# Polynomial attention and a blend of experts on one core: the first unit's queries by token, the third unit's rows behind the weights, the first copy of v in halves

## The chip, the cores and the metric

The program runs on one core of a Trainium2 chip. A core has five engines with a queue of instructions each: TensorE (PE; its weight loads are shown apart as PEld), VectorE (DVE), ScalarE (ACT), GpSimd (POOL) and SyncE (SP), which here issues nearly all transfers between the chip's memory and the core's. An engine takes its instructions strictly in the order of the program; between engines, semaphores say when something is done. The metric is the device time of one execution in microseconds (us); shown is the median of five.

## What is computed

Two blocks after one another, cut to what matters:

```python
# q, k, v: (4, 4, 1088, 32);  S1, S2: (8, 32)
def phi(x):                                  # 64 features of a row
    a = einsum('rd,bhsd->bhsr', S1, x)       # 8 numbers
    b = einsum('rd,bhsd->bhsr', S2, x)       # 8 numbers
    return einsum('bhsi,bhsj->bhsij', a, b)  # all 64 products
kv = einsum('bhsf,bhsd->bhfd', phi(k), v)
z  = phi(k).sum(axis=2)
x  = (phi(q) @ kv) / (phi(q) . z + 1e-6)     # then (b, h, s, d) -> (b*s, h*d): 4352 rows of 128

p = domain_probs / (domain_probs.sum(-1) + 1e-9)        # 4352 x 4
out = sum over e of p[:, e] * (relu(x @ w1[e]) @ w2[e]) # 4 experts, 128 -> 1024 -> 128
```

There is no softmax: a batch's keys and values shrink to one 64 x 33 table per head (kv and z), and each query is then a product with that table.

## The kernel before

**Order of the whole.** The 4352 tokens are cut into chunks of columns of x (128, 448, 512, five more of 512, 320, 256, 128), and a chunk goes through 16 steps, four for each expert: `first` multiplies by w1 and rectifies, `second`, two steps later, multiplies by w2. The attention makes x (`xT`, 128 features by 4352 tokens) in units of a batch: batch 0 in units of 128, 448 and 512 tokens. The order is written out by hand: `start()` makes keys, kv and the first unit of batch 0, and all later attention is cut into small pieces, which `work()` puts between the steps. So only the work of `start()` stands ahead of TensorE's expert products.

**Transfers (lines 85 to 163).** SP issues, in this order: S2, the keys of batch 0 (`kn`, 544 KB), q's first 128 columns (`qn`, 64 KB), v in four transfers of 128 KB and two of 16 KB, q's columns 128 to 1088 (480 KB; these are the second and third unit), w1[0], five small ones of domain_probs, w2[0], then w1 and w2 of experts 1 to 3, each 512 KB. Eight semaphores go round over the transfers, so that a transfer is issued only when the one eight before it has landed.

**Preparation.** VectorE decodes S (given as 64-bit words) into `s_T`, 32 x 64, by some fourteen small instructions. From it ScalarE and GpSimd lay out `sk`, the projection for the keys: 128 x 128, by head, S1 in one half and S2 in the other. They also lay out `sp` and from it `sr`, six 128 x 128 matrices, which are S1 and S2 with their rows already repeated in the order of the 64 products.

**`start()` (lines 674 to 733).** VectorE turns the rows of k (`kT`) and of the first 128 queries (`qT`) by blocks of 32. TensorE projects the keys in three groups of token tiles (0 to 3, 4 to 7, 8), token by feature, into PSUM tiles named `h`; ScalarE copies each group to `fs` (line 360). The products of the 64 features (`key_product`, line 391) are made by VectorE for the first pair of heads and by GpSimd for most of the second, into `kp`. ScalarE copies v into `vx`, which has a column of ones for z, in two copies of four tiles (line 337) and one of the last half tile (line 342). Then TensorE sums: `key_sum`, 36 instructions (72 records in the trace, where one instruction of this type shows as two) into one PSUM tile `f`, first tiles 0 to 3 for both pairs of heads, then 4 to 8.

The first unit's queries stand between the projections of the keys and the key sum. TensorE multiplies `qT` by the six matrices of `sr`, feature by token: the result in `o0` is the second factor of all products, that in `o1` and `num` the first factors. ScalarE copies `o0` to `qb`, and four VectorE products of 64 x 128 (line 501) give `qp`, 128 features by 128 tokens for each pair of heads.

At the end VectorE turns the second unit's rows (line 488, one instruction of 256 columns and one of 192), `key_divide` makes `kvz` from `f` between the two, TensorE multiplies `kvz` and `qp` to denominators (`den`) and numerators (`num`), VectorE divides into `xT` in two halves, and the expert products begin (`h` from `xT` and `w_sb`). The program's names w1_sb and w2_sb both show as `w_sb`. For chunk 0 the steps alternate on TensorE: eight records `h`, eight records `o`. Step 8 is the first that uses w1 of expert 2.

Of the kernel before, what the change touches and what calls it, by code (L numbers as in the profile page):

```python
# [8 lines left out]
F32 = mybir.dt.float32  # L9
BF16 = mybir.dt.bfloat16  # L10
I32 = mybir.dt.int32
ALU = mybir.AluOpType
# [4 lines left out]
def _ap(t, p0: int, np_: int, off: int, free):  # L17

    p = list(t.ap)[0]
    return bass.AP(t.tensor, t.offset + p0 * p[0] + off, [[p[0], np_]] + [list(d) for d in free])  # L20
# [3 lines left out]
def kernel(  # L24
# [24 lines left out]
    nc = tc.nc  # L49

    P = 128
# [32 lines left out]
    def psum(pool, tag):  # L84
        return pool.tile([P, 512], F32, tag=tag, name=tag)


    def load_rows(src, b, name, part=slice(0, S)):

        d = kn if name == "kn" else qn  # L90
        if b not in d:
            d[b] = lpool.tile([P, S], F32, tag=name, bufs=2, name=name)
        c, n = part.start, part.stop - part.start
        base = src.offset + b * H * S * D
        if name == "qn" and b == B - 1:
            for c, n, t in ((0, (G - 4) * D, 0), ((G - 4) * D, 4 * D, S - P)):
                nc.sync.dma_start(d[b][:, c : c + n], bass.AP(src.tensor, base + t * D, [[S * D, H], [n, 32], [1, n]]))
        else:
            nc.sync.dma_start(d[b][:, part], bass.AP(src.tensor, base + c, [[G * D, P], [1, n]]))  # L99
# [32 lines left out]
    def load_w2(e):  # L132
        nc.sync.dma_start(w2_sb[:, e], w2[e].rearrange("(f p) d -> p f d", p=P))  # L133
# [11 lines left out]

    ends = cpool.tile([P, 2, E], F32, name="ends")
    e_sum = cpool.tile([P, 2, 3], F32, name="e_sum")
    load_rows(q, 0, "qn", slice(P, S))
    load_w1(0)
    for p0, n, g0, m, t in ((0, 96, 0, G, 0), (96, 32, 0, G - 4, 3 * S), (96, 32, G - 4, 4, B * S - P)):  # L150
        nc.sync.dma_start(
# [8 lines left out]
    for e in range(1, E):  # L160
        load_w1(e)
        load_w2(e)
    sk = cpool.tile([P, P], F32, name="sk")
    sp = cpool.tile([32, 3, 2, 32], F32, name="sp")
    sr = cpool.tile([P, 3, 2, P], F32, name="sr")
    sq = cpool.tile([P, P], F32, name="sq")
    nc.gpsimd.memset(sk[:, :], 0.0)
    nc.gpsimd.memset(sr[:, :, :, :], 0.0)
    nc.gpsimd.memset(sq[:, :], 0.0)
    kT = cpool.tile([P, P * NT], F32, name="kT")  # L170
    nc.gpsimd.memset(kT[:, S:], 0.0)
# [6 lines left out]
    for h in range(H):  # L178
        nc.gpsimd.memset(own2[32 * h : 32 * h + 32, h % 2 : h % 2 + 1], 1.0)


    eps = cpool.tile([P, 1], F32, name="eps")
    nc.gpsimd.memset(eps[:, :], 0.0)
# [20 lines left out]
    def both(out, weights, moving, **flags):  # L204

        for _ in range(2):
            on_side(lambda s: out[half[s], :], lambda s: weights[:, half[s]], lambda s: moving, **flags)
# [34 lines left out]

    def copy_on(scalar):
        return nc.scalar.copy if scalar else nc.gpsimd.tensor_copy

    for h in range(H):
        copy_on(h < 2)(_ap(sk, 32 * h, 32, R2 * h, [[HP, 2], [1, R2]]), _ap(s_T, 0, 32, 0, [[D, 2], [1, R2]]))  # L250
    for i in range(3):
        copy_on(i == 2)(
            _ap(sp, 0, 32, HP * i, [[32, 2], [R, 4], [1, R]]),
            _ap(s_T, 0, 32, 4 * (i - 1) if i else R, [[D, 2]] + ([[1, 4], [0, R]] if i else [[0, 4], [1, R]])),
        )
    for h in range(H):
        copy_on(h > 1)(_ap(sr, 32 * h, 32, 32 * h, [[P, 6], [1, 32]]), _ap(sp, 0, 32, 0, [[32, 6], [1, 32]]))
    mask_lo = [R2 + l % R2 for l in range(32)]
    mask_b = [R + l % R for l in range(32)]
    mask_a = [[4 * x + l // R for l in range(32)] for x in range(2)]  # L260
# [72 lines left out]
            nc.vector.transpose(kT[:, 1024:S], kn[b][:, 1024:S])  # L333

    def value_copy(b):
        for r in range(2):
            nc.scalar.copy(
                vx[:, 4 * r : 4 * r + 4, :, 0:D].rearrange("p t h d -> p h t d"),
                _ap(vn[b], 0, P, P * r, [[8 * D, H], [D, 4], [1, D]]),
            )  # L340
            yield
        nc.scalar.copy(vx[0:64, 8, :, 0:D], _ap(vn[b], 0, 64, 1024, [[D, H], [1, D]]))

    def key_project(b, gi, kf):

        t0, n = FG[gi]
        if gi == 0:
            fss[b] = apool.tile([P, 2, NT, 32], F32, tag="fs", name="fs")
            kps[b] = apool.tile([P, NT, 2, P], F32, tag="kp", name="kp")
        for t in range(n):  # L350
            for i in range(2):
                for _ in range(2):
                    on_side(
                        lambda s: _ap(kf, HP * s, HP, 32 * t, [[P, 2], [1, 32]]),
                        lambda s: kT[:, P * (t0 + t) + HP * s : P * (t0 + t) + HP * s + HP],
                        lambda s: sk[:, HP * i : HP * i + HP],
                        start=(i == 0),
                        stop=(i == 1),
                    )
        nc.scalar.copy(  # L360
            _ap(fss[b], 0, P, 32 * t0, [[32 * NT, 2], [1, 32 * n]]), _ap(kf, 0, P, 0, [[P, 2], [1, 32 * n]])
        )
# [25 lines left out]
    def key_product(b, t0, n, p, x, eng, kf=None):  # L388

        src, off = (kf, P * p) if kf is not None else (fss[b], 32 * (NT * p + t0))  # L390
        eng.tensor_tensor(  # L391
            out=_ap(kps[b], 0, P, 256 * t0 + P * p + 64 * x, [[256, n], [32, 2], [R, 4], [1, R]]),
            in0=_ap(src, 0, P, off + 4 * x, [[32, n], [R2, 2], [1, 4], [0, R]]),
            in1=_ap(fss[b], 0, P, 32 * (NT * p + t0) + R, [[32, n], [R2, 2], [0, 4], [1, R]]),
            op=ALU.mult,
        )

    def key_sum(b, p, kv, t0=0, n=NT):
        for t in range(t0, t0 + n):
            both(  # L400
                kv[:, 256 * p : 256 * p + 2 * (D + 1)],
                kps[b][:, t, p, :],
                vx[:, t, 2 * p : 2 * p + 2].rearrange("p h d -> p (h d)"),

                start=(p == t == 0),
                stop=(t == NT - 1),
                skip_group_check=True,
            )
# [88 lines left out]
    def query_tiles():  # L497
        return [apool.tile([P, QW], F32, tag=f"qp{p}", name=f"qp{p}") for p in range(2)]

    def query_product(qp, p, x, n, qa, qb):  # L500
        nc.vector.tensor_tensor(  # L501
            out=qp[p][64 * x : 64 * x + 64, 0:n],
            in0=qa[64 * p : 64 * p + 64, 0:n],
            in1=qb[64 * p : 64 * p + 64, 0:n],
            op=ALU.mult,
        )
# [167 lines left out]
    def start():  # L674


        b, n = 0, UNITS[0][0]
        kf = []
        for t0 in (0, 2):
            key_turn(b, 0, t0, 2)  # L680
        for r in (1, 2):
            key_turn(b, r)
        qT = query_turn(b, 0, n)
        for gi in range(3):
            kf.append(psum(ps_h, "h"))
        value = value_copy(b)
        key_project(b, 0, kf[0])
        key_project(b, 1, kf[1])
        next(value)
        key_project(b, 2, kf[2])  # L690
        for _ in value:
            pass
        fq = [psum(ps_o, "o0"), psum(ps_o, "o1"), psum(ps_n, "num")]
        for i in range(3):
            for j in range(2):
                both(fq[i][:, 0:n], sr[:, i, j, :], qT[:, 0:n], start=(j == 0), stop=(j == 1))
        qb = apool.tile([P, QW], F32, tag="qb", name="qb")
        nc.scalar.copy(qb[:, 0:n], fq[0][:, 0:n])
        for x in range(2):
            key_product(b, 0, 4, 0, x, nc.vector, kf[0])  # L700
            key_product(b, 0, 4, 1, x, nc.gpsimd)
        for x in range(2):
            key_product(b, 4, 4, 0, x, nc.vector, kf[1])
            key_product(b, 8, 1, 0, x, nc.vector, kf[2])
        key_product(b, 4, 5, 1, 0, nc.gpsimd)
        key_product(b, 8, 1, 1, 1, nc.gpsimd)
        key_product(b, 4, 4, 1, 1, nc.vector, kf[1])
        kv = psum(ps_f, "f")
        for t0, n0 in ((0, 4), (4, 5)):
            for p in range(2):  # L710
                key_sum(b, p, kv, t0, n0)
        qp = query_tiles()
        for x in range(2):
            for p in range(2):
                query_product(qp, p, x, n, fq[1 + x], qb)
        for h in range(H):
            nc.gpsimd.tensor_copy(_ap(sq, 32 * h, 32, 32 * h, [[R2, 2], [1, R2]]), _ap(s_T, 0, 32, 0, [[D, 2], [1, R2]]))

        n1 = UNITS[b][1]
        qT = apool.tile([P, QW], F32, tag="qT2", name="qT2")  # L720
        turns = query_turns(b, n, n1, qT)
        next(turns)
        key_divide(b, kv)
        for _ in turns:
            pass
        first = attend_first(b, 0, n, qp)
        next(first)
        early[b, n] = psum(ps_o, "o1")
        both(early[b, n][:, 0:n1], sq[:, :], qT[:, 0:n1], start=True, stop=True)
        for _ in first:  # L730
            pass
        key_blocks(b, kv)
        gate_sums()
# [315 lines left out]
```

## Time and profile before

| | |
|---|---|
| five runs | 487.64, 487.77, 487.84, 487.95, 488.10 us; median 487.84 |
| the profiled execution | 487.64 us, its span 485.9 us |
| granted TensorE clock | 1.0 throughout |
| SP issues w1[0] | 5.40 us |
| SP issues w2[0], w1[1], w2[1], w1[2] | 9.44, 10.85, 12.13, 12.55 us |
| SP issues w2[2], w1[3], w2[3] | 13.17, 13.77, 15.88 us |
| first projection of keys on TensorE | 5.41 us |
| first expert product | 13.16 us |
| first expert product of expert 2 (step 8) | 19.83 us |

The span runs from the first to the last instruction of the execution that the profiler watched; times of single instructions count from its start. A row of the timeline gives start, length, engine, line, operation, the tile written and the tiles read, sizes and how many such instructions follow one another; in square brackets the time that the engine stood idle before and who released it. Matmuls are pipelined and their ends are modelled, so their starts are surer than their ends. A landing is the last of the 16 counts that a transfer adds to its semaphore.

### The profile page before, as it was taken

The numbers are of one execution on the slowest core, as the hardware profiler recorded it, in microseconds if no ns is written. First come the engines' busy times: TensorE is split into PE (matmuls) and PEld (weight loads), VectorE is DVE, ScalarE is ACT, GpSimd is POOL, SyncE is SP. The second block draws the span as 40 slices with busy tenths as digits, with TensorE's granted clock in tenths as the row PEclk, the third lists the DMA queues.
The fourth block names the chain that finished last, engine by engine and source line by source line (L and its number), as shares of the span: only waits on it lengthen the run. The fifth ranks groups of instructions, "written<-read, shape, count | busy, mean of one in ns | idle before, by whom it ended". The sixth has DMA issues, their size and how long they took to land.

```text
span 485.9 us, 11377 instructions
## 1 busy us (share of the span) xinstructions
PE 481.3 (99%) x4551; PEld 362.7 (75%) x4551; DVE 321.0 (66%) x759; ACT 246.8 (51%) x496; POOL 230.0 (47%) x270
## 2 busy tenths in 40 slices
PE   8999999999999999999999999999999999999997
PEld 6965666667777777777777777677777777999997
DVE  6859675686766668486776757668684666665642
ACT  4354564445544555355445555445455555566651
POOL 5172654435444455415455444424555445555571
PEclk9999999999999999999999999999999999999999
DMA  7990050211003123021103100021101200120000
GB/s 208 293 291 17 23 154 8 80 28 45 2 9 106 24 69 93 3 89 20 40 1 130 24 12 1 3 86 24 34 0 56 50 1 0 45 54 6 15 3 18
DMA packets 37772, 26.25 MB, mean 54 GB/s; under 512 B 24824, under 2 KB 34520, under 8 KB 37208
## 3 DMA queue, kind: packets, MB, share of 16 engines
q1 hardware_dynamic: 37704, 25.53, 18.8%
q8 instruction: 36, 0.59, 0.5%
q14 instruction: 16, 0.13, 0.1%
q10 hardware_dynamic: 16, 0.00, 0.0%
HBM read 21.28 MB, written 4.24 MB: 53 GB/s over the span
## 4 chain that ended last, share of the span: by engine, by line
PE 95%; DMA 3%; SPq 1%; issue 0%; DVE 0%
PE h L202 49%; PE o L202 40%; PE f L202 3%; DMA w_sb<-in_moe_w_dram 3%; PE den L202 2%; PE num L202 0%; SPq L105 0%; SPq L99 0%; SPq L110 0%; SPq L125 0%; SPq L133 0%; DVE end L856 0%
## 5 line engine op out<-in xcount | busy, mean ns | idle before, releaser
L202 PE MATMUL h<-xT,w_sb 128*64 128x512 f32 (+5 forms) x1424 | 298.8, 491 | 0.2 <-DMA w_sb<-in_moe_w_dram 0.2
L786 DVE SCALAR_TENSOR_TENSOR hid<-h,hid 128x256 f32<-128x256 f32 (+6 forms) x432 | 203.7, 472 | 143.3 <-ACT hid L817 134.9
L817 ACT ACTIVATE hid<-h 128x512 f32<-128x512 f32 (+3 forms) x288 | 158.4, 550 | 192.4 <-PE h L202 146.2
L202 PE MATMUL o<-hid,w2s 128*64 128x256 f32 (+3 forms) x1152 | 224.0, 355 | 0.0
L202 PEld LDWEIGHTS h<-xT,w_sb 128*64 128x64 f32 x1424 | 146.3, 137 | 50.6 <-issue 6.5
L202 PE MATMUL o<-hid,w_sb 128*64 128x256 f32 (+3 forms) x864 | 183.7, 355 | 0.0
L202 PEld LDWEIGHTS o<-hid,w2s 128*64 128x64 f32 x1152 | 132.3, 137 | 28.8
L930 POOL TENSOR_TENSOR ev<-yz,sh 64x256 f32<-64x256 f32 (+3 forms) x72 | 48.7, 676 | 159.9 <-ACT sh L933 157.2
L202 PEld LDWEIGHTS o<-hid,w_sb 128*64 128x64 f32 x864 | 100.5, 137 | 25.2 <-issue 5.8
L918 POOL TENSOR_TENSOR yz<-ev 128x512 f32<-128x512 f32 (+3 forms) x36 | 41.8, 1160 | 60.5 <-ACT ev L921 60.3
L930 POOL TENSOR_TENSOR ct<-ev 128x512 f32<-128x512 f32 (+3 forms) x36 | 42.5, 1182 | 2.8
L930 POOL TENSOR_TENSOR total<-total,ct 128x512 f32<-128x512 f32 (+3 forms) x27 | 31.9, 1180 | 2.1
L930 POOL TENSOR_TENSOR ct<-ct,gate 128x512 f32<-128x512 f32 (+3 forms) x27 | 31.8, 1176 | 2.1
L501 DVE TENSOR_TENSOR qp<-qa,qb 64x512 f32<-64x512 f32 (+5 forms) x44 | 30.1, 684 | 1.0
L920 ACT COPY ev<-o 128x512 f32<-128x512 f32 (+3 forms) x36 | 19.4, 539 | 12.7 <-PE o L202 12.3
L202 PE MATMUL o<-w_sb,hid 128*64 128x128 f32 x256 | 21.3, 273 | 0.0
L921 ACT COPY ev<-o 128x512 f32<-128x512 f32 (+3 forms) x36 | 19.4, 539 | 2.0
L202 PEld LDWEIGHTS o<-w_sb,hid 128*64 128x64 f32 x256 | 17.1, 137 | 1.6 <-issue 0.9
L809 ACT ACTIVATE hid<-h 128x256 f32<-128x256 f32 x23 | 8.4, 385 | 18.4 <-PE h L202 18.0
L391 DVE TENSOR_TENSOR kp<-fs 128x256 f32<-128x256 f32 (+1 forms) x24 | 16.7, 698 | 0.1
L933 ACT COPY sh<-yz 64x256 f32<-64x256 f32 (+3 forms) x36 | 13.7, 380 | 1.7 <-POOL yz L918 0.8
L202 PEld LDWEIGHTS den<-kvx,qp 128*64 128x64 f32 x240 | 12.3, 137 | 2.6 <-issue 0.5
(129 smaller groups left out, 246.4 us busy)
## 6 DMA issues: line engine op xcount, KB each, us to landing
w_sb<-in_moe_w_dram SPq DMA_DIRECT2D x8, 512.0 KB, 6.7
gate<-gates SPq DMA_DIRECT2D x4, 1024.0 KB, 4.7
kn<-in_k_dram SPq DMA_DIRECT2D x4, 544.0 KB, 6.9
vn<-in_v_dram SPq DMA_DIRECT2D x16, 128.0 KB, 3.4
gate<-gates SPq DMA_DIRECT2D x2, 896.0 KB, 5.9
qn<-in_q_dram SPq DMA_DIRECT2D x2, 544.0 KB, 3.8
out_dram<-ob SPq DMA_DIRECT2D x16, 64.0 KB, 2.0
qn<-in_q_dram SPq DMA_DIRECT2D x2, 480.0 KB, 5.9
```

Of the source, the lines that this page charges most:

```text
L202: nc.tensor.matmul(out(s), weights(s), moving(s), **flags)
L391: eng.tensor_tensor(out=_ap(kps[b], 0, P, 256 * t0 + P * p + 64 * x, [[256, n], [32, 2], [R, 4], [1, R]]), in0=_ap(src, 0, P, off + 4 * x, ...
L501: nc.vector.tensor_tensor(out=qp[p][64 * x : 64 * x + 64, 0:n], in0=qa[64 * p : 64 * p + 64, 0:n], in1=qb[64 * p : 64 * p + 64, 0:n], op=A ...
L786: nc.vector.scalar_tensor_tensor(out=out, in0=src, scalar=0.0, in1=in1, op0=ALU.max, op1=ALU.subtract)
L809: nc.scalar.activation(hd[:, 0 : 2 * n], hp[:, 0 : 2 * n], ACTF.Relu)
L817: nc.scalar.activation(hd[:, n * j : n * j + n], hp[:, 0:n], ACTF.Relu)
L918: add = lambda out, in0, in1, op=ALU.add: nc.gpsimd.tensor_tensor(out=out, in0=in0, in1=in1, op=op)
L920: nc.scalar.copy(_ap(ev, 0, P, 0, [[2 * w, 2], [1, w]]), _ap(a0, 0, P, 0, two))
L921: nc.scalar.copy(_ap(ev, 0, P, w, [[2 * w, 2], [1, w]]), _ap(a1, 0, P, 0, two))
L930: add = lambda out, in0, in1, op=ALU.add: nc.gpsimd.tensor_tensor(out=out, in0=in0, in1=in1, op=op)
L933: nc.scalar.copy(sh[HP:P, 0:w], yz[0:HP, 0, 0:w])
```

## The change

Three things are changed, all in the first microseconds of the program.

*The first unit's queries.* `sp` and `sr` go. TensorE projects the 128 queries as it does the keys, token by feature, with `sk`: four instructions of 64 columns into `num`. ScalarE copies this to `qs`, and VectorE makes all products by token with two instructions of 128 x 128 into `qt`. To get features by token again, TensorE multiplies `qt` with a unit matrix (`ident`), four instructions of 128 columns into `o0`, placed between the key sums of tiles 4 to 8 for the first and the second pair of heads. ScalarE copies the result to `qp2`, which takes the place of `qp`. The unit matrix is built at the start: VectorE fills `diag` (five memsets, then five shuffles that double the columns), GpSimd clears `ident` and copies four blocks of 32 x 32 into it. For the key sum of tiles 0 to 3 nothing changes; the last key product on VectorE now comes behind the two of `qt`.

*The rows of q.* The transfer of columns 128 to 1088 is split: columns 128 to 576 (the second unit, 224 KB) keep the place, columns 576 to 1088 (the third unit, 256 KB) are issued behind w1[1] and w2[1], and so ahead of w1[2].

*v.* For batch 0 the first copy of v into `vx` is cut into two, heads 0 and 1, heads 2 and 3. The first of them is issued on ScalarE between the copies `fs` of the first and the second group of keys, the second between those of the second and the third group. The second copy of four tiles comes behind the third `fs`, and the one of the last half tile behind `qs`. For other batches the copies stay as they were.

```diff
-    load_rows(q, 0, "qn", slice(P, S))
+    load_rows(q, 0, "qn", slice(P, P + UNITS[0][1]))
     load_w1(0)
...
     for e in range(1, E):
         load_w1(e)
         load_w2(e)
+        if e == 1:
+            load_rows(q, 0, "qn", slice(P + UNITS[0][1], S))
...
-    sp = cpool.tile([32, 3, 2, 32], F32, name="sp")
-    sr = cpool.tile([P, 3, 2, P], F32, name="sr")
-    nc.gpsimd.memset(sr[:, :, :, :], 0.0)
...
+    ident = cpool.tile([P, P], F32, name="ident")
+    nc.gpsimd.memset(ident[:, :], 0.0)
+
+    diag = cpool.tile([P, 32], F32, name="diag")
+    nc.vector.memset(diag[:, 0:1], 0.0)
+    for h in range(H):
+        nc.vector.memset(diag[32 * h : 32 * h + 1, 0:1], 1.0)
+    for d in (1, 2, 4, 8, 16):
+        nc.vector.stream_shuffle(in_=diag[:, 0:d], out=diag[:, d : 2 * d], mask=[(l - d) % 32 for l in range(32)])
...
-    for i in range(3):
-        copy_on(i == 2)(
-            _ap(sp, 0, 32, HP * i, [[32, 2], [R, 4], [1, R]]),
-            _ap(s_T, 0, 32, 4 * (i - 1) if i else R, [[D, 2]] + ([[1, 4], [0, R]] if i else [[0, 4], [1, R]])),
-        )
     for h in range(H):
-        copy_on(h > 1)(_ap(sr, 32 * h, 32, 32 * h, [[P, 6], [1, 32]]), _ap(sp, 0, 32, 0, [[32, 6], [1, 32]]))
+        copy_on(False)(ident[32 * h : 32 * h + 32, 32 * h : 32 * h + 32], diag[32 * h : 32 * h + 32, :])
...
     def value_copy(b):
-        for r in range(2):
+
+        for r, h, n in ((0, 0, 2), (0, 2, 2), (1, 0, 4)) if b == 0 else ((0, 0, 4), (1, 0, 4)):
             nc.scalar.copy(
-                vx[:, 4 * r : 4 * r + 4, :, 0:D].rearrange("p t h d -> p h t d"),
-                _ap(vn[b], 0, P, P * r, [[8 * D, H], [D, 4], [1, D]]),
+                vx[:, 4 * r : 4 * r + 4, h : h + n, 0:D].rearrange("p t h d -> p h t d"),
+                _ap(vn[b], 0, P, P * r + 8 * D * h, [[8 * D, n], [D, 4], [1, D]]),
             )
             yield
...
         key_project(b, 0, kf[0])
+        next(value)
         key_project(b, 1, kf[1])
         next(value)
         key_project(b, 2, kf[2])
+
+        fq = psum(ps_n, "num")
+        for i in range(2):
+            for _ in range(2):
+                on_side(
+                    lambda s: fq[half[s], 0:HP],
+                    lambda s: qT[:, HP * s : HP * s + HP],
+                    lambda s: sk[:, HP * i : HP * i + HP],
+                    start=(i == 0),
+                    stop=(i == 1),
+                )
+        next(value)
+        qs = apool.tile([P, HP], F32, tag="qs", name="qs")
+        nc.scalar.copy(qs[:, :], fq[:, 0:HP])
         for _ in value:
             pass
-        fq = [psum(ps_o, "o0"), psum(ps_o, "o1"), psum(ps_n, "num")]
-        for i in range(3):
-            for j in range(2):
-                both(fq[i][:, 0:n], sr[:, i, j, :], qT[:, 0:n], start=(j == 0), stop=(j == 1))
-        qb = apool.tile([P, QW], F32, tag="qb", name="qb")
-        nc.scalar.copy(qb[:, 0:n], fq[0][:, 0:n])
...
+        qt = apool.tile([P, 2, P], F32, tag="qt", name="qt")
+        for x in range(2):
+            nc.vector.tensor_tensor(
+                out=_ap(qt, 0, P, 64 * x, [[P, 2], [32, 2], [R, 4], [1, R]]),
+                in0=_ap(fq, 0, P, 4 * x, [[32, 2], [R2, 2], [1, 4], [0, R]]),
+                in1=_ap(qs, 0, P, R, [[32, 2], [R2, 2], [0, 4], [1, R]]),
+                op=ALU.mult,
+            )
         key_product(b, 4, 4, 1, 1, nc.vector, kf[1])
         kv = psum(ps_f, "f")
-        for t0, n0 in ((0, 4), (4, 5)):
-            for p in range(2):
-                key_sum(b, p, kv, t0, n0)
-        qp = query_tiles()
-        for x in range(2):
-            for p in range(2):
-                query_product(qp, p, x, n, fq[1 + x], qb)
+        for p in range(2):
+            key_sum(b, p, kv, 0, 4)
+        key_sum(b, 0, kv, 4, 5)
+
+        tq = psum(ps_o, "o0")
+        for p in range(2):
+            both(tq[:, P * p : P * p + P], qt[:, p, :], ident[:, :], start=True, stop=True)
+        key_sum(b, 1, kv, 4, 5)
+        qp2 = apool.tile([P, 2 * P], F32, tag="qp2", name="qp2")
+        nc.scalar.copy(qp2[:, :], tq[:, 0 : 2 * P])
+        qp = [qp2[:, P * p : P * p + P] for p in range(2)]
```

## The prediction

> **What bounds the kernel now.** I read three views in this order: the page for the whole run, the chain of waits for the place where TensorE stops being the bound, and the timeline of the first 20 us, where all edits lie. The page first (busy time and share of an engine; then the chain that ended last):
>
> ```profile
> PE 481.3 (99%) x4551; PEld 362.7 (75%) x4551; DVE 321.0 (66%) x759; ACT 246.8 (51%) x496; POOL 230.0 (47%) x270
> PE 95%; DMA 3%; SPq 1%; issue 0%; DVE 0%
> ```
>
> TensorE is the bound nearly everywhere; 3% of the chain is transfers. Where those 3% lie, the chain in order of time says (start, length, what):
>
> ```profile
> 5.40 6.71 DMA w_sb<-in_moe_w_dram
> 12.13 0.38 SPq L133
> 12.55 7.15 DMA w_sb<-in_moe_w_dram
> 19.70 0.14 issue
> 19.83 0.66 PE h L202 x8
> ```
>
> Up to 19.83 us the end is set by weights, not by the start of the attention. w1[0], issued at 5.40, lands at 12.11; the queue lets a new transfer go only when the one eight before it has landed, so w2[1] is issued at 12.13, w1[2] right behind at 12.55, and w1[2] lands at 19.70. TensorE needs it for step 8 of the first chunk (expert 2) and starts at 19.83. From there to 485.9 the chain is TensorE without a hole, so what moves 19.83 moves the end one for one, and what does not move it is worth nothing. How early could TensorE be there?
>
> ```profile
> 18.60 0.61 PE L202 MATMUL h<-xT,w_sb 128*64 128x128 f32 x8
> 19.03 0.61 PE L202 MATMUL o<-w_sb,hid 128*64 128x128 f32 x8
> 19.83 0.66 PE L202 MATMUL h<-xT,w_sb 128*64 128x128 f32 x8 [0.19 <-DMA w_sb<-in_moe_w_dram]
> ```
>
> Groups of eight start 0.43 to 0.44 apart, so step 8 would have started at 19.03 + 0.44 = 19.47: w1[2] already costs 0.36 us, and a shorter start only adds to that wait. The start itself, from the last key projections to the first expert product:
>
> ```profile
> 7.53 0.37 ACT L360 COPY fs<-h 128x256 f32<-128x256 f32 x1 [0.56 <-PE h L202]
> 7.53 1.07 PE L202 MATMUL o<-qT,sr 128*64 128x128 f32 x16
> 8.41 0.64 PE L202 MATMUL num<-qT,sr 128*64 128x128 f32 x8
> 8.84 2.30 PE L202 MATMUL f<-vx,kp 128*64 128x66 f32 x72
> 10.86 0.45 DVE L488 STREAM_TRANSPOSE qT<-qn 128x256 f32<-128x256 f32 x1 [0.16 <-DMA qn<-in_q_dram]
> 11.33 0.49 DVE L414 TENSOR_TENSOR kvz<-f,own 128x128 f32<-128x128 f32 x2
> 13.16 1.65 PE L202 MATMUL h<-xT,w_sb 128*64 128x64 f32 x48
> ```
>
> **The change, part by part.**
>
> *Query products (start).* Out go 24 TensorE records (16 `o`, 8 `num`), which push the key sum `f` from 7.53 to 8.84: 1.31 us, or 0.055 each. In come 8 records of 64 columns, priced as the key sum's 72 records between 8.84 and 10.91, 0.029 each: 0.23; and 8 of 128 columns, 8 x 0.055 = 0.44. TensorE saves 0.64, but the sum is no longer one run: the 8 `ident` records stand in the middle of it and wait for VectorE.
>
> *v in two halves.* The order on ScalarE becomes fs, half of vx, fs, half, fs, vx. The half stands ahead of the second fs copy, in the 0.56 us that ScalarE idles before 7.53. But it needs all of v's four large transfers, and the DMA view of the fourth (its issue at 3.50 alone) says 4.0 to landing, so 7.5:
>
> ```profile
> vn<-in_v_dram SPq DMA_DIRECT2D x1, 128.0 KB, 4.0
> ```
>
> ScalarE thus waits there to about 7.57. Steps from the timeline's starts: a 128x256 copy 0.27 (7.53 to 7.80), a 128x512 one 0.53, the small fs 0.10. Half 7.57, second fs 7.84, half 8.11, third fs 8.38, vx 8.48, `qs` 9.01 to 9.22 (a 128x64 copy, 0.21). Queued behind the second fs is line 391's product of tiles 4 to 7, which slips from 7.94 to 8.25; VectorE's next three (1.02 for four at 8.57, less the last 0.42) start at 8.60 and end by 9.20. Then two `qt` at 9.26, priced as the two `kvz`, 0.49: 9.75. TensorE's `ident` records 9.81 to 10.25; the last 20 records of the sum, 20 x 0.029 = 0.58, issue until 10.83, against 10.91 now. The last key product, 0.42 from 9.75, is ready at 10.17, in time. `qp2`, one 128x256 copy at 10.3, is done before `den` needs it.
>
> *After the sum.* `kvz` stood behind the turn of the second unit's rows, which waited for its transfer (10.86). With 224 KB in place of 480 KB that lands earlier, VectorE is free at 10.17, the turn is over before the sum is, and `kvz` starts at 11.14 + 0.03 - 0.08 = 11.09 in place of 11.33. So the first expert product comes about 0.25 earlier (12.9). Bounds: 0 if the rows land no earlier; 0.45 if v lands early enough that the second fs keeps 7.53 (0.31 back, less what TensorE then takes).
>
> *Preamble.* VectorE gets five memsets and five shuffles ahead of the decoding of S. Shuffles of 512, 448 and 128 columns take 738, 659 and 295 ns: 0.15 fixed plus 1.15 ns a column, so 0.15 to 0.17, with 0.03 between dependent ones 0.95; memsets at 0.11 (the one of `s_hl`) 0.55. 0.81 + 1.5 + 0.11 = 2.42, where VectorE waited for S until 2.39. Nothing, then; if it were more, 0.77 us of idle before the first projection (TensorE's weight load at 5.38) still cover it. GpSimd loses 0.74 (sr) and two copies of sp and two of sr, and gets one memset and four copies at 0.24: free again at 5.6, its next work is at 7.12. ScalarE loses one copy of sp and two of sr before 5.8: it was idle after them.
>
> *Third unit's rows.* They are needed at 24.46 and land by about 18: covered by 6 us. What counts is the queue. SP's order becomes qn (448 columns), w1[0], gates' inputs, w2[0], w1[1], w2[1], qn (512), w1[2]. Everything up to w2[1] has 256 KB fewer ahead of it; w1[2] has exactly the same bytes ahead of it as before, plus one more issue (0.43) on SP. 256 KB at the 320 to 377 GB/s of the windows from 14 to 20 us is 262 KB / 345 = 0.76 us. If the queue is never empty before w1[2], its landing does not move (0). If the gap in the middle cannot be used, w1[2] comes 0.76 later. The gap is there:
>
> ```profile
> 10.00:11.00 1.00, 1.00 (x41) 1.00 (x39) 0.81 (x4) 0.00 (x0) 0.55 (x4) 1.00 0.57 144
> 11.00:12.00 1.00, 0.68 (x15) 0.44 (x13) 0.97 (x4) 0.00 (x0) 0.00 (x0) 1.00 0.59 161
> 18.00:19.00 1.00, 1.00 (x23) 1.00 (x20) 0.94 (x3) 0.39 (x1) 0.17 (x1) 1.00 1.20 331
> ```
>
> (last column GB/s). It follows from w2[0]'s late issue at 9.44, behind the slow issues of domain_probs, which this change leaves alone. But a transfer has landed only with its last of 16 counts, and in the trace's semaphore events one count trails: of w1[2] the fifteenth comes at 18.77, the sixteenth at 19.70; of qn 9.41 and 10.84; of w1[0] 11.09 and 12.11. That last sixteenth works through the gap without pause, so for it only bytes count: 19.70 again, plus about 0.1 for one more transfer in smaller rows. The other fifteen: 18.77 + 0.76 = 19.53, still earlier. I take +0.1; ends -0.3 (the trailing sixteenth loses its lag, and the others set 19.4 to 19.5) and +0.76.
>
> A rule that speaks against the split: the Trainium skill, page "DMA: Bandwidth & Descriptors", section Bandwidth, wants transfers batched to 1 MiB or more, and its section on the anatomy of one DMA puts about 2.0 us fixed cost on each. The row here: kn and the first rows of q, issued at 1.20 and 1.62, land 3.6 and 3.5 us later, one right behind the other, so fixed costs overlap. If the rule's cost fell on the queue whole, w1[2] would land at 21.7 and the run take some 489.8; by the row it does not.
>
> **Sum.** Step 8 is ready at 19.47 - 0.25 = 19.22 but waits for w1[2]: 19.83 + 0.1. The profiled execution takes 487.64 (span 485.9 and 1.74 around it), the median of the five runs is 487.84; + 0.1 on the median gives 487.9. The 0.25 of the start, and TensorE's 0.64, vanish in a longer wait for w1[2].
>
> **Rivals.** (1) *The gain comes through.* The trailing count is a matter of this execution, w1[2] lands by 19.4 and step 8 starts near 19.4: 0.4 to 0.5 gained, 487.4; with the start's best 0.45, 0.36 + 0.45 = 0.81, so 487.0. For it: w1[0] and w2[1] are freed 256 KB earlier. Against: bytes ahead of w1[2] are the same. (2) *The third unit's rows push w1[2]* by the full 0.76: 488.6. For it the gap at 10 to 12; against it the trailing count. A further lag of the sixteenth count like the one it shows (19.70 less 18.77, 0.93) would take it to 489.5. (3) *Preamble late, clearly slower.* If tiny shuffles and memsets cost as the 448-column one, 0.66, five plus five memsets 3.85, that is 2.4 past VectorE's 1.46 of waiting; 0.77 is covered, 1.6 delays projections, and step 8 is ready at 20.8 to 21.1: 488.8 to 489.1. It decides once the preamble exceeds 1.46 + 0.77 + 0.61 = 2.8 us. Against: the fit of the shuffle rows. (4) *The reordering does nothing at the start*: the wait on v takes back all of TensorE's 0.64 and more; by the wait's slack of 0.36 this is again 487.8 to 488.0.
>
> **How the numbers follow.** Forecast with (4) 0.57, own range 487.6 to 488.3; (1) 0.20; (2) 0.13; (3) 0.06; something not listed 0.04. Range 487.2 to 488.7. A measurement of this kernel tells about 0.2%, 0.98 us, from no change: below 486.9 only the very best of (1) and the unlisted (0.08), above 488.8 most of (3) and the tail of (2) (0.16), the rest, 0.76, within.
>
> **What would show it.** Right: the second fs copy starts after 7.53, behind a wait for v; `kvz` near 11.1 and the first expert product near 12.9; step 8 at 19.7 to 20.0 with a longer idle before it, released by w_sb. Wrong: step 8 without a wait (then the start decides), the projections starting later than 5.41, or a difference that arises after 20 us.

## The result, and the profile after

The changed kernel takes 488.68 us (median of 28 runs, 487.61 to 490.14); the kernel before, in 49 runs beside them, 487.88. The ratio is 1.0015, interval 1.0008 to 1.0021: 0.4 to 1.0 us slower, 0.73 in the middle. That is inside the range of the forecast, 0.02 below its upper end, and within its 0.2%, but it is 0.8 above the forecast, and the interval lies clear of 1.

The 0.73 can be cut in two with the spans. Those of the 49 runs are not on record, so the changed kernel's (28 runs and the profiled one) are set against the 86 runs of the kernel before that stand beside the experiments below. The mean span rose by 0.48 us (two standard errors: 0.28), from 486.18 to 486.66. The shortest tenth of the spans hardly moved (it ends at 485.7 before, 485.8 after); the longest tenth did (it begins at 486.85 and 487.6). The time outside the span, run time less span, rose from 1.79 to 2.03 (medians). The forecast had a term for the first part only.

The profiled execution of the changed kernel took 489.04 us, span 487.0. First the page, busy time by engine and the chain that ended last:

```profile
PE 481.4 (99%) x4543; PEld 363.0 (75%) x4543; DVE 320.7 (66%) x772; ACT 246.0 (51%) x495; POOL 229.3 (47%) x270
PE 95%; DMA 3%; SPq 2%; issue 0%; DVE 0%
```

TensorE is busy for the same time as before (481.4 against 481.3), so the 1.1 us by which this span is longer are a wait. The chain in order of time (start, length, what) shows where:

```profile
3.51 4.37 DMA vn<-in_v_dram
7.89 0.67 SPq L156
8.61 0.58 SPq L156
9.23 1.41 SPq L133
10.69 0.59 SPq L130
11.32 0.43 SPq L133
11.80 1.37 SPq L99
13.21 8.02 DMA w_sb<-in_moe_w_dram
21.23 0.14 issue
21.37 0.66 PE h L210 x8
```

The place is the one that the forecast named, w1[2] ahead of step 8. Its landing moved from 19.70 to 21.23 and step 8 from 19.83 to 21.37. The rows before it show that SP was long over two issues: w2[0] (line 133) took 1.41 us, where the kernel before needed 0.43, and the third unit's rows (line 99) 1.37. The row of w2[0] in the kernel before:

```profile
9.44 0.43 SPq L133 DMA_DIRECT2D w_sb<-in_moe_w_dram  x1
```

TensorE's timeline after the change puts a price on it:

```profile
19.35 0.61 PE L210 MATMUL o<-w_sb,hid 128*64 128x128 f32 x8
21.37 0.66 PE L210 MATMUL h<-xT,w_sb 128*64 128x128 f32 x8 [1.41 <-DMA w_sb<-in_moe_w_dram]
```

With steps 0.44 apart TensorE could have gone on at 19.79: 1.58 us are lost, where before it was 0.36. The start, on ScalarE and then VectorE:

```profile
7.97 0.41 ACT L340 COPY vx<-vn 128x256 f32<-128x256 f32 x1 [0.73 <-DMA vn<-in_v_dram]
8.29 0.36 ACT L363 COPY fs<-h 128x256 f32<-128x256 f32 x1
```

```profile
9.74 0.49 DVE L721 TENSOR_TENSOR qt<-num,qs 128x128 f32<-128x128 f32 x2
10.47 0.43 DVE L491 STREAM_TRANSPOSE qT<-qn 128x256 f32<-128x256 f32 x1
11.57 0.49 DVE L417 TENSOR_TENSOR kvz<-f,own 128x128 f32<-128x128 f32 x2 [0.66 <-PE f L210]
```

The first half of v waits for its transfer and holds up the second fs copy, as foretold; `kvz` no longer stands behind the turn of the rows but waits 0.66 for the key sum. The first expert product starts at 13.47 (before 13.16). All of that lies later by 0.27 to begin with, because `kn` landed at 5.07 and not at 4.80.

At 10 to 12 us the gap in the transfers, which before was at 144 and 161 GB/s, was deeper in this execution (stretch, TensorE and the other engines, clock, DMA share, GB/s):

```profile
10.00:11.00 1.00, 1.00 (x34) 1.00 (x32) 0.91 (x4) 0.01 (x1) 0.84 (x5) 1.00 0.07 6
11.00:12.00 1.00, 0.75 (x23) 0.53 (x18) 0.43 (x3) 0.36 (x1) 0.41 (x4) 1.00 0.32 63
```

### The profile page after: what moved, and what is told of

It reads as the page before. It is cut to its first block, busy times and chain, and to the rows that moved or that the text cites. A ratio compares the mean times of both kernels' runs of the same rounds, so it can differ in the third digit from the quotient of the medians.

```text
span 487.0 us, 11373 instructions
## 1 busy us (share of the span) xinstructions
PE 481.4 (99%) x4543; PEld 363.0 (75%) x4543; DVE 320.7 (66%) x772; ACT 246.0 (51%) x495; POOL 229.3 (47%) x270
## 4 chain that ended last, share of the span: by engine, by line
PE 95%; DMA 3%; SPq 2%; issue 0%; DVE 0%
PE h L210 49%; PE o L210 40%; PE f L210 3%; PE den L210 2%; DMA w_sb<-in_moe_w_dram 2%; DMA vn<-in_v_dram 1%; PE num L210 1%; SPq L99 0%; SPq L133 0%; SPq L105 0%; SPq L156 0%; SPq L130 0%; SPq L125 0%; DVE end L880 0%
```

## The experiments

Two theories stood against each other. By the forecast's own, the new place of the third unit's rows costs w1[2] about nothing and the new start is worth nothing while w1[2] decides. By the rival, the rows push w1[2] by up to 0.76. The runs take the two halves of the change apart, look at both kernels a second time, and then take the wait for w1[2] away, so that the new start alone would decide. "Outside" is the median of run time less span; the span's difference is to the kernel before in the runs beside it (for the changed kernel, to the 86 runs), with two standard errors.

| run | median us | ratio, 95% | span, difference of means | outside |
|---|---|---|---|---|
| the changed kernel | 488.68 | 1.0015 [1.0008, 1.0021] | +0.48 ± 0.28 | 2.03 |
| e1_third_rows_behind_w1_3 | 488.24 | 1.0004 [0.9995, 1.0013] | −0.08 ± 0.30 | 1.99 |
| e2_rows_in_one_transfer | 488.15 | 1.0005 [0.9996, 1.0013] | +0.02 ± 0.27 | 2.06 |
| e3_old_start_rows_split | 487.72 | 1.0002 [0.9992, 1.0011] | −0.02 ± 0.37 | 1.79 |
| e4_old_start_rows_behind_w1_3 | 487.99 | 1.0002 [0.9994, 1.0011] | +0.03 ± 0.27 | 1.78 |
| e5_changed_weights_first | 488.33 | 1.0008 [0.9997, 1.0018] | +0.25 ± 0.46 | 2.02 |
| e6_before_weights_first | 487.82 | 0.9994 [0.9986, 1.0003] | −0.18 ± 0.28 | 1.79 |
| e7_before_three_w1_first | 489.05 | 1.0021 [1.0012, 1.0029] | +1.05 ± 0.21 | 1.79 |
| e8_new_start_three_w1_first | 489.41 | 1.0028 [1.0017, 1.0038] | +0.96 ± 0.20 | 2.18 |
| f1_before_v_in_halves | 488.01 | 1.0000 [0.9990, 1.0009] | +0.06 ± 0.28 | 1.80 |
| f2_before_with_preamble | 488.31 | 1.0010 [0.9999, 1.0022] | +0.37 ± 0.55 | 1.92 |

r1_changed_again and r2_before_again were one run each, for their traces: 487.51 (span 485.7, outside 1.81) and 488.32 (span 486.5, outside 1.82).

### The rows of q, with the new start and with the old one

On the changed kernel, the third unit's rows go behind w1[3] (e1), or the split is undone (e2):

```diff
 # e1
         load_w1(e)
-        load_w2(e)
-        if e == 1:
+        if e == E - 1:
             load_rows(q, 0, "qn", slice(P + UNITS[0][1], S))
+        load_w2(e)
 # e2
-    load_rows(q, 0, "qn", slice(P, P + UNITS[0][1]))
+    load_rows(q, 0, "qn", slice(P, S))
...
-        if e == 1:
-            load_rows(q, 0, "qn", slice(P + UNITS[0][1], S))
```

> The changed kernel with one thing moved: the third unit's rows are issued behind w1[3] in place of behind w2[1], so nothing new stands ahead of w1[2] and 256 KB fewer than before do. If those rows push w1[2] (theory): w1[2] lands near 18.7 to 19.3, step 8 starts without a long wait at 19.2 to 19.6, and the run takes 487.0 to 487.5. If the loss sits in the start of the attention (rival: wait for v, preamble): step 8 still late, 488.4 to 489. If only the trailing sixteenth count of w1[2] decides, whatever stands ahead of it: 487.8 to 488.0.

> The changed kernel with the rows of q in one transfer of 480 KB as before; queries by token and v in halves stay. Theory (the loss is the place of the third unit's rows): 487.8 to 488.0, step 8 at 19.8 as in the kernel before. Rival (the loss is in the start): 488.4 to 489.

On the kernel before, the split alone, with the third unit's rows where the change puts them (e3) or behind w1[3] (e4):

```diff
 # e3
-    load_rows(q, 0, "qn", slice(P, S))
+    load_rows(q, 0, "qn", slice(P, P + UNITS[0][1]))
...
         load_w2(e)
+        if e == 1:
+            load_rows(q, 0, "qn", slice(P + UNITS[0][1], S))
 # e4, the same with
         load_w1(e)
+        if e == E - 1:
+            load_rows(q, 0, "qn", slice(P + UNITS[0][1], S))
         load_w2(e)
```

> The kernel before with the split of the rows alone, third unit's rows ahead of w1[2] as in the change. Theory: the whole loss of the change is here, 488.4 to 489.0, step 8 at 20.5 to 21.4 after a wait for w_sb. Rival (start): 487.6 to 488.0.

> The kernel before with the rows split and the third unit's part behind w1[3]. If w1[2] lands 0.4 or more earlier, step 8 is set by the start at about 19.4 to 19.5: 487.4 to 487.6. Against the first run of this call it shows what the new start by itself is worth once no weight is waited for: theory 0 to 0.3 less for the new start; rival (the new start is slower) this one is faster than the first run.

With the new start, taking the rows out from ahead of w1[2] brings the span back to that of the kernel before (−0.08 and +0.02 against +0.48). With the old start, putting them there costs nothing (−0.02 ± 0.37). The two statements don't fit well together: with the new start the rows cost 0.48 less −0.03 (mean of e1 and e2), 0.51, with the old one −0.02 less 0.03, −0.05; the 0.56 between these has two standard errors of 0.57, by those in the table. So it is not shown that the new start and the rows hurt only together; a cost of the rows of some 0.2 to 0.3 with either start lies within the intervals as well. No time fell where the theory of these expectations had put it: e1 and e2 came out above its ranges, e3 below, and e4 above.

### Each kernel once more

> The changed kernel itself, a second profile. In the first one SP's issue of w2[0] took 1.41 us (0.43 before) while one of the 16 engines fetched 16 KB of instructions, and w1[2] landed at 21.2. If that meeting belongs to the program: the issue is long again, w1[2] lands at 20.8 to 21.5. If it is an accident of the execution: the fetch stands elsewhere and w1[2] lands at 19.7 to 20.4, as its 256 KB more ahead of it make it.

> The kernel before itself, a second profile, for how far landings move from one execution to another: kn at 4.8 to 5.4, w1[2] at 19.3 to 20.3, first expert product 8.2 to 8.5 after kn has landed.

No edit. The changed kernel's second trace has neither the long issue nor the long wait. SP's timeline and TensorE's:

```profile
9.04 0.43 SPq L133 DMA_DIRECT2D w_sb<-in_moe_w_dram  x1
9.70 0.39 SPq L130 DMA_DIRECT2D w_sb<-in_moe_w_dram  x1
11.03 0.38 SPq L133 DMA_DIRECT2D w_sb<-in_moe_w_dram  x1
11.45 0.63 SPq L99 DMA_DIRECT2D qn<-in_q_dram  x1
12.12 0.74 SPq L130 DMA_DIRECT2D w_sb<-in_moe_w_dram  x1
```

```profile
19.16 0.61 PE L210 MATMUL o<-w_sb,hid 128*64 128x128 f32 x8
19.68 0.66 PE L210 MATMUL h<-xT,w_sb 128*64 128x128 f32 x8
```

w2[0]'s issue takes 0.43 instead of 1.41, the third unit's rows 0.63 instead of 1.37, and step 8 starts at 19.68 instead of 21.37, only 0.08 later than the 0.44 of a step allow. The span is 485.7, shorter than that of the kernel before. From 10 to 12 us the transfers run at 79 and 262 GB/s, where the first trace had 6 and 63: the deeper gap came with the long issue (e1, whose w2[0] issue was long too, has 2 and 59) and not with the change. The kernel before, for its part, has in its second trace a long issue of w1[1] and loses time at step 8:

```profile
9.78 1.53 SPq L130 DMA_DIRECT2D w_sb<-in_moe_w_dram  x1
...
20.43 0.64 PE L202 MATMUL h<-xT,w_sb 128*64 128x128 f32 x7 [0.49 <-DMA w_sb<-in_moe_w_dram]
```

So the 1.58 us lost in the first trace of the changed kernel are no measure of the change: the same program is 1.3 us apart in two traces. What the change does has to be read across traces. These are the ten in which the order of the weights is the same, from their semaphore events and records (counts of 16; us):

```text
                 w2[0]                      w1[2], counts            step 8  span
                 issue  length first count  first  15th   16th
third unit's rows ahead of w1[2]
  changed         9.23  1.41   14.14        19.25  20.37  21.23      21.37   487.0
  changed, r1     9.04  0.43   12.76        17.96  19.05  19.55      19.68   485.7
  e3              8.96  0.43   12.46        17.84  19.44  19.68      19.87   485.8
not ahead of it
  before          9.44  0.43   13.16        17.52  18.77  19.70      19.83   485.9
  before, r2      9.30  0.43   12.99        17.83  19.27  20.30      20.43   486.5
  e1              9.58  1.37   14.25        18.70  19.50  20.32      20.46   486.4
  e2              9.19  0.42   12.82        17.11  18.87  18.95      19.75   485.9
  e4              9.27  0.43   12.99        17.20  19.70  19.73      20.39   486.5
  f1              9.21  0.43   12.98        17.18  18.40  18.55      19.85   486.1
  f2              9.43  0.43   13.03        17.72  20.20  20.27      20.98   486.7
```

Three things can be read here. The span less step 8 is 465.6 to 466.2 in all ten, while step 8 itself moves by 1.7: most of the difference in span is decided by then. From w2[0]'s first count to w1[2]'s it takes 5.10, 5.19, 5.38 with the rows between them (mean 5.23) and 4.20 to 4.84 without (mean of seven 4.43): the 256 KB cost 0.79 of streaming, and the two groups don't overlap. And w2[0]'s first count comes 3.50 to 3.77 after its issue wherever that issue was short, with 256 KB fewer ahead of it (r1 3.72, e3 3.50) or not (before 3.72): what the change took out of the queue ahead of w2[0] brought this count no nearer to the issue.

That the 0.79 don't show in full in the times may lie with the sixteenth count; no run tests this. It follows the fifteenth by 0.03 to 1.03 in these ten, and only the sixteenth releases step 8, which starts 0.13 to 0.14 behind it wherever it waits. In r1 and e3 the fifteenth counts, at 19.05 and 19.44, came before TensorE could use them, and the last ones trailed by 0.50 and 0.25; in the kernel before it was 0.93 and 1.03.

In e3 step 8 did not wait for w1[2] at all, because TensorE had already waited for w1[1], which landed at 16.22 (before 15.70), at step 4:

```profile
16.35 0.66 PE L204 MATMUL h<-xT,w_sb 128*64 128x128 f32 x8 [0.30 <-DMA w_sb<-in_moe_w_dram]
...
19.87 0.64 PE L204 MATMUL h<-xT,w_sb 128*64 128x128 f32 x8
```

### Weights ahead of the probabilities

The five slow issues of domain_probs stand ahead of w2[0] and make the gap. In e5 (changed) and e6 (before) two weights go past them:

```diff
     load_w1(0)
+    load_w2(0)
+    load_w1(1)
     for p0, n, g0, m, t in ((0, 96, 0, G, 0), (96, 32, 0, G - 4, 3 * S), (96, 32, G - 4, 4, B * S - P)):
...
-    load_w2(0)
     for e in range(1, E):
-        load_w1(e)
+        if e > 1:
+            load_w1(e)
         load_w2(e)
```

> The changed kernel with the five transfers of domain_probs moved behind w1[1], so that w2[0] and w1[1] are issued at 6 to 7 us in place of 9.2 and 10.7. If late weights are the loss: w1[2] lands by 18, no step waits for a weight, step 8 stands 6.3 behind the first expert product and the run takes 487.2 to 487.6. If the start is the loss: 488.2 to 488.7 all the same.

> The kernel before with the same move of domain_probs. No weight is waited for here either, so against the run with the new start this one shows what the start alone is worth. By the prediction's step the new start is 0.25 faster: this run 487.4 to 487.7, 0.2 to 0.3 above the other. By the rival (the wait for v on ScalarE takes it back): equal within 0.1, or this one faster.

Neither came to the first range named for it (487.2 to 487.6 and 487.4 to 487.7). In e5 the two weights were issued at 5.89 and 6.41, but then the order by eights held up what came behind: w2[1] went out at 11.43, when w1[0] had landed (11.41), the rows at 13.08 (w2[0] landed 13.06), w1[2] at 14.67 (w1[1] landed 14.65). w1[2] landed at 19.80, and step 8 lost 0.41. Its 488.33 lies in the range named for a loss in the start, but since a weight was waited for, e5 against e6 does not show what the start alone is worth. In e6, without the additional transfer in the queue, w1[2] went out at 12.90, landed at 18.38 and was not waited for; the span is 0.18 ± 0.28 shorter. Of all kernels tried it is the only one with a ratio below 1, and its interval takes in 1.

### No wait for w1[2]

In e7 (before) and e8 (changed, rows in one transfer) w1[2] too goes past the probabilities; these are then read two steps later.

```diff
     load_w1(0)
+    load_w2(0)
+    for e in range(1, 3):
+        load_w1(e)
+        if e == 1:
+            load_w2(e)
...
-    load_w2(0)
-    for e in range(1, E):
-        load_w1(e)
-        load_w2(e)
+    load_w2(2)
+    load_w1(3)
+    load_w2(3)
...
-            if i == 2:
+            if i == 4:
                 gate_quotients()
-            elif i == 5:
+            elif i == 6:
                 store_gates()
```

> The kernel before with the weights up to w1[2] issued ahead of the five transfers of domain_probs; the quotients of the gates and their store one or two steps later, so that VectorE does not wait for them. If the wait for weights between 16 and 20 us is what both kernels pay: w1[2] lands at 17 to 18.3, step 8 stands 6.3 behind the first expert product, mean span 485.6 to 485.8 (486.1 before), 487.3 to 487.6. If weights are no longer what counts: 487.8 to 488.0.

> The changed kernel with the rows of q in one transfer and the same order of weights. Against the run before it in this call it is the new start alone, without waits for weights. If the start is a draw: first expert product 8.2 to 8.4 after kn's landing in both, spans equal within 0.15; the time outside the span, 2.03 against 1.78 in the runs so far, puts it 0.25 above. By the prediction's step (0.25 earlier) its span is 0.25 shorter.

Both lost a microsecond. w1[2] landed at 18.09 and 18.46, and step 8 came without a wait, but domain_probs was now late. VectorE in e7 and in e8, then TensorE in e7:

```profile
19.69 0.25 DVE L283 TENSOR_SCALAR e_sum<-e_sum 128x2 f32<-128x2 f32 x1 [1.03 <-POOL e_sum L274]
20.31 0.25 DVE L283 TENSOR_SCALAR e_sum<-e_sum 128x2 f32<-128x2 f32 x1 [1.71 <-POOL e_sum L274]
```

```profile
19.60 0.61 PE L206 MATMUL h<-xT,w_sb 128*64 128x128 f32 x8
...
21.66 0.57 PE L206 MATMUL den<-kvx,qp 128*64 128x66 f32 x12 [0.58 <-DVE qp L505]
...
23.63 0.61 PE L206 MATMUL h<-xT,w_sb 128*64 128x128 f32 x8
```

VectorE stood 1.03 us (in e8 1.71) for the sums of domain_probs, with the second unit's query products queued behind; TensorE waited for those at `den`, and step 10 began at 23.63 (before 22.54), 1.09 later, which is the 1.05 of the span. A wait was put in the place of the one removed. So the pair does not show what the new start is worth: its spans differ by 0.96 − 1.05 = −0.09, with two standard errors of about 0.3, but in both kernels the end is set by domain_probs, and behind that wait an earlier start would not show.

### Two parts of the new start alone

f1 has only v in halves, on the kernel before; f2 has only the building of the unit matrix, which nothing then uses.

```diff
 # f1
-        for r in range(2):
+        for r, h, n in ((0, 0, 2), (0, 2, 2), (1, 0, 4)) if b == 0 else ((0, 0, 4), (1, 0, 4)):
...
         key_project(b, 0, kf[0])
+        next(value)
         key_project(b, 1, kf[1])
 # f2
+    ident = cpool.tile([P, P], F32, name="ident")
+    nc.gpsimd.memset(ident[:, :], 0.0)
...
+    for d in (1, 2, 4, 8, 16):
+        nc.vector.stream_shuffle(in_=diag[:, 0:d], out=diag[:, d : 2 * d], mask=[(l - d) % 32 for l in range(32)])
...
+    for h in range(H):
+        copy_on(False)(ident[32 * h : 32 * h + 32, 32 * h : 32 * h + 32], diag[32 * h : 32 * h + 32, :])
```

> The kernel before with the copies of v in halves alone. In the span: ScalarE waits for v, the second fs copy starts 0.3 to 0.5 later after kn's landing, and since TensorE works through the query products meanwhile the first expert product moves by 0 to 0.3. Outside the span: 2.03 if the 0.25 belongs to this part, 1.78 if not.

> The kernel before with the making of the unit matrix (five memsets and five shuffles on VectorE, one memset and four copies on GpSimd) put in on top, its result unused. In the span nothing moves by more than 0.2. Outside the span: 2.03 if the 0.25 belongs to this part, 1.78 if not; if neither this run nor the one with v in halves shows it, it belongs to the query products.

The halves change nothing, in the span (+0.06 ± 0.28) or outside it (1.80), although f1's second fs copy starts 3.07 after `kn` has landed, behind a wait for v, and not 2.73 after it as before. f2 is inconclusive for the span: +0.37 ± 0.55, with one run of ten at 490.61. Outside the span it has 1.92, half of the way from 1.78 to 2.03.

## Why the prediction was right or wrong

488.68 lies in the range by 0.02, and it is made up of two parts that the sum did not have, so that it lies inside is in good part luck. It is also near rival (2)'s 488.6, but a third of the loss is time outside the span, which is not that rival's mechanism. Of the prediction's own signs of being right, the second fs copy behind a wait for v came true; step 8 (21.37 and, in r1, 19.68) and the first expert product (13.47) did not.

**Which wait decides: right in most executions.** In eight of the ten traces with the old order of the weights a weight holds up TensorE at step 4 or 8; in e2 and f1 none is late, and TensorE's own pace decides. The span follows step 8 to within 0.3 us either way.

**The start's 0.25: wrong, and worth about nothing.** From `kn`'s landing to the first expert product the old start took 8.36, 8.22, 8.23, 8.46, 8.25 and 8.23 us (before, r2, e3, e4, e6, e7) and the new one 8.40, 8.38, 8.37, 8.29, 8.24 and 8.29 (after, r1, e1, e2, e5, e8). The steps one by one, the changed trace less the 0.27 of `kn`: v's last large transfer at 7.60 (7.5 foretold), the second fs at 8.02 (7.84), `qt` at 9.47 (9.26), `kvz` at 11.30 (11.09; before 11.33). So the gain of `kvz` was 0.03 and not 0.24. `kvz` is now released by the key sum, as foretold, but its wait for the rows was that of one trace: there the rows' sixteenth count came at 10.83, in r2 at 9.29. In r2, e3, e6, e7 and f2 the old start has `kvz` 6.40 to 6.42 after `kn`, with VectorE at work without a pause before it; in the first trace it was 6.53, in e4 6.64, and with the new start it is 6.35 to 6.50. The mis-sized term is ScalarE's order: v came 0.10 later and the half copy with the fs behind it took the rest, so that the last key sum started 0.12 later than before where the forecast had it 0.08 earlier. Rival (4), that the reordering does nothing, is what the traces show up to the first expert product. The forecast of step 8 did not rest on it.

**The preamble: right.** Its five shuffles took 0.15 to 0.17 each, and it was done at 2.35; VectorE then still waited 0.16 for S and began to decode it at 2.51 instead of 2.39. The projections began at 5.68 and not at 5.41, one of the prediction's signs of being wrong, but that is `kn`'s landing: in every trace, with the preamble or without, they begin 0.61 or 0.62 after it. Rival (3) is out.

**The third unit's rows, +0.1: the step that failed.** It rested on "w1[2] has exactly the same bytes ahead of it as before" and on the sixteenth count, which "works through the gap without pause, so for it only bytes count". The bytes ahead are the same, but the 256 KB were taken from before the gap, where they delayed nothing that w2[0] waited for, and put behind it, where they cost 0.79 in the mean of three traces (w2[0]'s first count to w1[2]'s). This is the price of rival (2), 0.76, and its mechanism, for the first counts. For the landing it holds only in part: the sixteenth count did not go by bytes alone, its distance from the fifteenth moved between 0.03 and 1.03 from execution to execution. In the times it is 0.48 ± 0.28 with the new start and −0.02 ± 0.37 with the old; why these differ, if they do, is open. One rival was not tested: w2[0]'s issue was long in two of the four traces with the new start and this order of weights (changed, e1) and in none of the six with the old start. If the new start brings the long issue on more often, that would lengthen some executions and leave others alone, as the spans of the changed kernel do.

**The split's fixed cost.** The Trainium skill (page "DMA: Bandwidth & Descriptors", section on the anatomy of one DMA) gives a fixed cost of about 2.0 us for a DMA, fitted on DMAs that GpSimd issues; here SP issues them. The prediction's estimate of 489.8 for the split goes by that figure. e3 and e4, which split the rows and do nothing else, came to −0.02 ± 0.37 and +0.03 ± 0.27: no run shows such a cost.

**The 1.74 around the span: a missing term.** The sum took it as fixed. Its median is 1.78 to 1.80 in every timed kernel with the old start but f2, and 1.99 to 2.18 in every one with the new start. In the changed kernel it is 0.24 more, a third of the whole loss, and for e1 and e2, whose spans equal those of the kernel before, all of it (488.24 and 488.15 against 487.77 beside them). The rows' split (e3, e4), the order of the weights (e6, e7) and v in halves (f1) are not its cause; building the unit matrix seems to bring half of it (f2). What it consists of no view shows. The one run of r1, at 1.81, is at the low end of what the changed kernel's runs have, 1.79 to 2.13.

So the time came out at 488.68 rather than 487.9: 0.48 in the span, of which the forecast had 0.1, and 0.24 outside, of which it had nothing.

## What to carry to other kernels

Bytes moved within a transfer queue are not neutral because their sum ahead of a late load stays the same: look for the gap first. Here 256 KB ahead of it delayed nothing that was waited for, and behind it they cost their 0.79 of streaming at the first counts, if not always in the time. Work taken off an engine at the start is worth something only if no other wait takes it back (here that for v did) and no load decides, and taking the load's wait away by reordering may only hand the wait to what was pushed back (domain_probs in e7 and e8). Where a single landing sets the end, one trace of each kernel is not a comparison, and a wait that stands in one trace may be that execution's alone (`kvz` for the rows): take the chain from several executions, and the difference in time from spans and totals separately.

## What the runs showed that was not expected

- The issue of one 512 KB weight or of the rows, between 9 and 12 us, took 0.3 to 1.0 us in most traces and 1.3 to 1.5 us for one or two of them in six of ten (changed, e1, e3, e4, r2, f2). Where it was w2[0]'s, the data came later by about as much: its first count 4.91 and 4.67 after an issue of 1.41 and 1.37 (changed, e1), else 3.50 to 3.77. It does not come in every execution of one program (r1 does not have it). Near it lies a 16 KB fetch of instructions of about 1 us, beginning at 9.15 to 10.98 in these traces, but four traces have the fetch in that stretch and no long issue (before, r1, e2, f1), so the cause was not found.
- `kn`, the first large transfer, landed at 4.80 to 5.44 us in traces that differ up to there only in small preparations on VectorE, GpSimd and ScalarE, and at 4.80 and 5.25 in two of one program; this alone moves the whole start by 0.64.
- The time outside the span, 1.78 to 2.18 us, differs between kernels that differ only in their first microseconds.
